# Fourteen remainders of converted weights on GpSimd instead of VectorE

## The chip, the cores and the metric

The kernel runs on one core of a Trainium2 chip. The metric is the device time of one execution in microseconds (us). TensorE does the matrix products, VectorE (DVE), ScalarE (ACT) and GpSimd (POOL) work on tiles in SBUF, SyncE (SP) issues the DMAs. VectorE and ScalarE also read PSUM, where TensorE writes.

## The reference

Channel attention over 6016 tokens of 256 channels, and after it two dense layers, each with a wide hidden part of 2048:

```
qn = q / (norm(q, axis=1) + 1e-6); kn = k / (norm(k, axis=1) + 1e-6)
a  = softmax(kn^T @ qn / tau)          # 256 x 256
x  = v @ a                             # 6016 x 256
h  = x @ w1_in;  g = elu(h);  x = g @ w1_out
h  = x @ w2_in;  g = silu(h); out = g @ w2_out
```

q, k and v are float32. The four weight matrices (256 x 2048 and 2048 x 256) are float64.

## The kernel before, in words

*Precision.* Each factor of a product is kept as two tiles: a high part, rounded to the type that TensorE takes at full rate (fp32r), and the remainder, the value less the high part. `product` issues three matmuls for one product: high x high, high x remainder, remainder x high, in this order, all into one PSUM bank (line 297). `split` (line 288) makes the pair: `copy(hi, src)` on ScalarE (line 256 in the profile), then `tt(lo, src, hi, subtract)` on VectorE (line 270). `products` (line 311) does the same for two products that share a bank.

*Conversion of the weights.* A float64 weight arrives as two 32-bit words. `in_f32` makes a float32 of them: two copies on ScalarE (tiles "cv" and "st"), then on VectorE two `tensor_scalar` operations (line 273, "cv<-cv"), a `scalar_tensor_tensor` (line 276, "cv<-st,cv") and an integer addition (line 270, shown as CUSTOM_DVE_ANT_0). `convert` then calls `split` with the float32 chunk of 128x512. The weights of layer one come in eight chunks of w_in ("w1i") and eight of w_out ("w1o"). Chunks 0 and 1 of w_in are split into corners of the tile "wo", the other six into "xs", all eight of w_out into "wo". So the remainders of layer one are `wo<-cv,wo` ten times and `xs<-cv,xs` six times. The weights of layer two are split by other functions (`put_by`, `second_weights`).

*Stages.* First the column norms and kn^T q are summed over all tokens while q and k are loaded (to about 41 us). Then the softmax, and the product of it with the chunks of w_in (`m_product`, `m_group`, line 311), which puts the attention into the weights of layer one. Tokens are then worked in groups of 1024 (the last of 896), all of layer one and then all of layer two, each group in eight steps `j` over the hidden part. In a step four units of 128x512 are made: `first_plain` in the first group (24 matmuls), a scheme with fewer products and more additions in all later ones. Each unit goes through the activation (`unit`, line 256 on ScalarE, lines 276 and 270 on VectorE) into a pair of tiles "gs", the last of which is the remainder `gs<-e,gs` on VectorE (where the pair lies in spare room of "wa", `wa<-e,wa`). `second` multiplies a unit with a chunk of w_out, six matmuls into the banks "y". In the first group (to about 160 us) the chunks of w_out and of w_in are converted as the steps need them: the conversions, the units and the products of the softmax with w_in run side by side there.

*Order.* All instructions are first put in a list by `do`, with an engine, a price from the table `COST` and the tiles they read and write. `in_order`, a planner, then writes one order for each engine by these prices and by the length of the way to the end; the engines run their orders strictly, with waits where tiles are shared. All DMAs go through SP's queue, but for some at the beginning and the end. GpSimd makes constants and the identity matrix in the first 1.3 us and nothing after.

Of the kernel before, what the change touches and what calls it, by code (L numbers as in the profile page):

```python
# [16 lines left out]
ALU = mybir.AluOpType  # L17
# [4 lines left out]
EARLY = ("w1i", 0), ("w1i", 1), ("w1o", 0), ("w1i", 2), ("w1i", 3)  # L22
# [21 lines left out]
    "PE": (0.0127, 1 / 2400, 0.22, 0.0),  # L44
    "ACT": (0.14, 1 / 1400, 0.18, 0.12),
    "DVE": (0.067, 1 / 960, 0.15, 0.19),
    "SP": (0.37, 0, 2.3, 0.0),
    "-": (0.0, 0, 0.0, 0.0),
}
# [2 lines left out]
V = namedtuple("V", "ap keys")  # L52
# [20 lines left out]
def real(ap):  # L73
    return ap.get() if isinstance(ap, Later) else ap
# [80 lines left out]
def channel_attention_elu_silu(  # L155
# [28 lines left out]
    nc = tc.nc  # L184
# [38 lines left out]
    def f32(ap):  # L223
        return ap.bitcast(F32)
# [6 lines left out]
    def do(engine, n, emit, reads, writes, times=1, far=0.0):  # L231
        fixed, each, late, own = DENSE if dense and engine == "ACT" else COST[engine]
        late += far
        ops.append(
            Op(
                engine,
                times * (fixed + each * n),
                late,
                own,
                emit,  # L240
                [k for v in reads if isinstance(v, V) for k in v.keys],
                [k for v in writes for k in v.keys],
                hot,
            )
        )

    def width(ap):
        return int(np.prod(ap.shape[1:]))

    def at(x):  # L250
        return real(x.ap) if isinstance(x, V) else x
# [14 lines left out]
    def copy(out, src, **kw):  # L266
        act(out, src, AF.Copy, **kw)

    def tt(out, a, b, op):
        do("DVE", width(out.ap), lambda: nc.vector.tensor_tensor(at(out), at(a), at(b), op), [a, b], [out])  # L270
# [14 lines left out]
        queue, engine = (nc.scalar, "ACT") if by == "ACT" else (nc.sync, "SP")  # L285
        do(engine, 0, lambda: queue.dma_start(at(out), at(src)), [src], [out], n if engine == "SP" else 2 + 3 * short, far)  # L286

    def split(hi, lo, src):
        copy(hi, src)
        tt(lo, src, V(f32(hi.ap), hi.keys), ALU.subtract)  # L290

    def product(out, lhs, rhs, start=True, stop=True, **kw):

# [90 lines left out]
    def wo_at(part, i):  # L384

        also = tuple(("eT", part, d) for d in range(CT)) if i == NP - 1 else ()
        if i in (5, 6):
            also = tuple(("w1i", part, x) for x in range(2))
        return V(wo[part][:, 2 * i : 2 * i + 2], (("wo", part, i), *also))

    def w1i_at(i, a, c, half=None):

        if i == 0:
            w = wo[a][:, 10:14].rearrange("p (c x) f -> p c (x f)", c=CT)
            return V(w[:, c], (("w1i", a, half),))
        x = 2 * ((i - 1) % 2)
        return V(xs[0][:, x : x + 2, a][:, c], (("x", x, a), ("x", x + 1, a)))
# [31 lines left out]
    def in_f32(name, i, *order, far=0.0, after=(), wait=()):  # L429


        raw = load(name, i, *order, far=far, after=after)
        low, high = src_of.pop((name, i))
        t = cvs.take()
        a, b = low.ap.shape[1:3]
        w = V(t.ap.rearrange("p (a b) -> p a b", a=a), t.keys)
        wi = V(w.ap.bitcast(I32), t.keys)
        copy(w, V(f32(high.ap), high.keys + wait), scale=2.0**-112)
        copy(low, V(low.ap.bitcast(U32), low.keys + wait), scale=2.0**-29)
        ts(w, w, TOP, -TOP, ALU.min, ALU.max)  # L440
        ts(wi, wi, 3, None, ALU.logical_shift_left)
        stt(wi, V(high.ap, high.keys), SIGN, wi, ALU.bitwise_and, ALU.bitwise_or)
        tt(V(flat(wi.ap), wi.keys), V(flat(wi.ap), wi.keys), V(flat(low.ap), low.keys), ALU.add)
        return w, raw

    def convert(name, i, *order, wait=(), far=LATE[0]):
        w, _ = in_f32(name, i, *order, far=far if order else 0.0, wait=wait)
        if name == "w1i":
            s = slice(i % 2 * HC, (i % 2 + 1) * HC)
            hi, lo = (w1i_at(i // 2, a, slice(None), i % 2) for a in range(2))  # L450
            split(V(hi.ap[:, :, s], hi.keys), V(lo.ap[:, :, s], lo.keys), w)
        else:
            split(wo_at(0, i), wo_at(1, i), w)

    def put_by(name, i, s):


        w, raw = in_f32(name, i, far=FAR, after=[("step", s - 1)])
        wf = V(flat(w.ap), w.keys)
        if name == "w2i":  # L460
            dma(V(w_dram[i], (("wid", i),)), wf)
            return
        both = V(raw.ap.rearrange("p (a x) -> p a x", a=2), raw.keys)
        half = lambda a: V(both.ap[:, a].bitcast(F32R), both.keys)
        split(half(0), half(1), wf)
        dma(V(wo_dram[i].rearrange("p a x r -> p a (x r)"), (("wod", i),)), both)
# [23 lines left out]
    with tc.manual_schedule():  # L490
# [87 lines left out]
        for i, (j0, nj) in enumerate(rows):  # L578
# [21 lines left out]
            if i == len(ENDS[0]):  # L600
                tau_ps = V(nsq.ap[:, 4:5], nsq.keys)
                matmul(tau_ps, V(ones, ()), V(small[:, 0:1], ("tau",)))
                recip(rtau, tau_ps)
        hot = 1
        convert(*EARLY[0], "order")
        hot = 0
        hot = 1
        convert(*EARLY[1], "order", far=LATE[1])
        hot = 0
        j0, nj0 = groups[0]  # L610
        for n in (1, 0):
            for b in range(4):
                s = slice(n * nj0 // 2, (n + 1) * nj0 // 2)
# [17 lines left out]
        for i in range(HELD[1] - 1, -1, -1):  # L631
            scores(last - i, (0,))
        hot = 0
        convert(*EARLY[2], "order")
        hot = 3
        x = V(nsq.ap[:, 0:4], nsq.keys)
# [617 lines left out]
```

## Time and profile before

| what | value |
|---|---|
| runs | 1037.50, 1037.96, 1038.38 us (median 1037.96) |
| profiled execution, span from first to last instruction | 1035.8 us |
| TensorE busy | 1030.4 us (99%) |
| VectorE busy | 825.1 us (80%) |
| ScalarE busy | 749.4 us (72%) |
| GpSimd busy | 0.7 us (0%) |
| granted TensorE clock | full speed throughout |

The span of the profiled execution is what the profile shows of its time; the median of the runs lies 2.2 us above it. Busy shares are means over stages: in 60 to 142 us VectorE is busy for 80.56 of 82 us, after 600 us for some 65 in 100. A group of matmuls in the timeline goes from the first one's start to the last one's end, and matmuls overlap, so twelve of them that follow each other at full rate take 2.88 us and not twelve times the duration of one. A group that holds a wait is longer than its like.

### The profile page before, as it was taken

Reading aid. Unit: us, or ns where it says so; the run is one execution under the profiler, and the core shown is the slowest. Engines: PE = TensorE matmul, PEld = TensorE weight load, DVE = VectorE, ACT = ScalarE, POOL = GpSimd, SP = SyncE. Lnnn points to the kernel's source line nnn. Section 1 sums busy time; section 2 is a strip of 40 time slices with the busy share of each in tenths; the row PEclk is TensorE's granted clock in tenths of the full one; section 3 lists DMA queues with packets and bytes.
Section 4 is the critical chain, followed back from the end, with each engine's and each line's share of the span. In section 5 each row is a group of like instructions: output and inputs, shape, how many; then the busy total and the mean of one; then the engine's idle time right before and its main releaser. Section 6 shows DMA issues by size and latency. Waiting matters only on the chain.

```text
span 1035.8 us, 13366 instructions
## 1 busy us (share of the span) xinstructions
PE 1030.4 (99%) x4734; PEld 872.4 (84%) x4734; DVE 825.1 (80%) x1401; ACT 749.4 (72%) x1410; POOL 0.7 (0%) x6
## 2 busy tenths in 40 slices
PE   9999999999999999999999999999999999999998
PEld 8888888888888888888998888998888888888887
DVE  6999999999989989989998866667566657657553
ACT  6799988989788888888897765565565556555543
POOL 0000000000000000000000000000000000000000
PEclk9999999999999999999999999999999999999999
DMA  9663332033032113013434003012003003001102
GB/s 379 220 173 113 112 71 102 1 72 112 18 75 103 51 46 102 31 42 122 135 97 156 11 1 82 1 41 37 1 4 78 1 1 82 1 1 22 20 1 41
DMA packets 112389, 71.38 MB, mean 69 GB/s; under 512 B 87874, under 2 KB 90562, under 8 KB 111682
## 3 DMA queue, kind: packets, MB, share of 16 engines
q1 hardware_dynamic: 109584, 68.96, 22.6%
q10 hardware_dynamic: 2738, 1.57, 0.5%
q8 instruction: 37, 0.61, 0.3%
q14 instruction: 30, 0.25, 0.1%
HBM read 49.81 MB, written 20.71 MB: 68 GB/s over the span
## 4 chain that ended last, share of the span: by engine, by line
PE 99%; ACT 0%; ACTq 0%; DVE 0%; issue 0%
PE y L297 50%; PE h L297 44%; PE y L324 4%; PE h L311 1%; PE h L324 0%; PE y L311 0%; PE h L329 0%; ACTq L286 0%; ACT big L256 0%; PE y L329 0%; ACT h L256 0%; ACT a L256 0%; DVE a L276 0%; DVE ones L491 0%; ACT e L256 0%
## 5 line engine op out<-in xcount | busy, mean ns | idle before, releaser
L297 PE MATMUL y<-gs,wo 128*128 128x512 f32 (+1 forms) x2196 | 520.5, 385 | 0.0
L297 PEld LDWEIGHTS y<-gs,wo 128*128 128x128 f32 x2196 | 411.8, 188 | 78.1 <-ACT e L256 0.8
L297 PE MATMUL h<-xs,wa 128*128 128x512 f32 (+1 forms) x1980 | 472.6, 385 | 0.0
L297 PEld LDWEIGHTS h<-xs,wa 128*128 128x128 f32 x1980 | 370.9, 188 | 68.5
L270 DVE TENSOR_TENSOR gs<-e,gs 128x512 fp32r<-128x512 f32 (+1 forms) x382 | 253.2, 676 | 90.9 <-ACT e L256 88.6
L270 DVE TENSOR_TENSOR h<-h,h 128x512 f32<-128x512 f32 (+1 forms) x352 | 228.0, 678 | 80.2 <-PE h L297 62.3
L256 ACT ACTIVATE e<-h 128x512 f32<-128x512 f32 (+2 forms) x383 | 225.5, 600 | 46.1 <-DVE h L270 43.5
L256 ACT ACTIVATE h<-h 128x512 f32<-128x512 f32 (+1 forms) x176 | 103.6, 589 | 136.8 <-PE h L297 136.7
L256 ACT ACTIVATE gs<-h 128x512 fp32r<-128x512 f32 (+1 forms) x192 | 116.5, 607 | 70.0 <-DVE h L270 37.7
L276 DVE SCALAR_TENSOR_TENSOR e<-e,h 128x512 f32<-128x512 f32 (+1 forms) x190 | 123.0, 671 | 18.2 <-ACT e L256 17.7
L256 ACT ACTIVATE e<-e 128x512 f32<-128x512 f32 (+1 forms) x192 | 114.0, 623 | 1.3
L256 ACT ACTIVATE gs<-e 128x512 fp32r<-128x512 f32 (+1 forms) x190 | 110.7, 624 | 1.6 <-DVE e L276 1.6
L270 DVE TENSOR_TENSOR xs<-big,xs 128x512 fp32r<-128x512 f32 (+1 forms) x77 | 50.2, 672 | 0.0
L256 ACT ACTIVATE xs<-big 128x512 fp32r<-128x512 f32 (+1 forms) x77 | 45.4, 623 | 1.0 <-DVE big L270 0.7
L270 DVE TENSOR_TENSOR sums<-sums 128x2048 f32<-128x2048 f32 (+3 forms) x17 | 29.4, 1727 | 7.2 <-ACT sums L256 6.2
L273 DVE TENSOR_SCALAR cv<-cv 128x512 f32<-128x512 f32 (+1 forms) x64 | 26.4, 422 | 0.6 <-ACT cv L256 0.3
L297 PEld LDWEIGHTS y<-wo,gs 128*128 128x128 f32 x192 | 24.7, 191 | 1.0
L297 PE MATMUL y<-wo,gs 128*128 128x256 f32 x192 | 25.1, 283 | 0.0
L256 ACT ACTIVATE cv<-st 128x512 f32<-128x512 f32 x32 | 21.4, 674 | 1.5 <-DMA st<-in_moe_w_in_dram 1.5
L324 PE MATMUL y<-ring 128*128 128x256 f32 x92 | 22.3, 395 | 0.0
L276 DVE SCALAR_TENSOR_TENSOR cv<-st,cv 128x512 int32<-128x512 int32 x32 | 21.9, 687 | 0.4
L270 DVE CUSTOM_DVE_ANT_0 cv<-st,cv 128x1024 uint16<-128x1024 uint16 x32 | 21.9, 686 | 0.0
(100 smaller groups left out, 369.6 us busy)
## 6 DMA issues: line engine op xcount, KB each, us to landing
st<-in_moe_w_in_dram SPq DMA_DIRECT2D x16, 512.0 KB, 3.9
st<-in_moe_w_out_dram SPq DMA_DIRECT2D x16, 512.0 KB, 3.8
yd<-e SPq DMA_DIRECT2D x20, 256.0 KB, 2.4
big<-yd SPq DMA_DIRECT2D x5, 1024.0 KB, 4.7
big<-in_v_dram SPq DMA_DIRECT2D x32, 128.0 KB, 3.5
wod<-st SPq DMA_DIRECT2D x8, 512.0 KB, 2.9
wo<-wod SPq DMA_DIRECT2D x8, 512.0 KB, 4.0
out_dram<-big SPq DMA_DIRECT2D x32, 128.0 KB, 2.9
```

The costliest lines, as they stand in the source:

```text
L256: nc.scalar.activation(at(out), at(src), func, **{k: at(x) for k, x in kw.items()}, **more)
L270: do("DVE", width(out.ap), lambda: nc.vector.tensor_tensor(at(out), at(a), at(b), op), [a, b], [out])
L273: do("DVE", width(out.ap) / 2, lambda: nc.vector.tensor_scalar(at(out), at(a), at(s1), at(s2), *op), [a, s1, s2], [out])
L276: emit = lambda: nc.vector.scalar_tensor_tensor(at(out), at(a), at(s), at(b), op0, op1)
L297: nc.tensor.matmul(at(out), at(lhs[a]), at(rhs[b]), start=start and a + b == 0, stop=stop and a == 1, **kw)
L311: nc.tensor.matmul(at(out), at(both[n][0][a]), at(both[n][1][b]), start=(n, a, b) == (0, 0, 0), stop=(n, a) == (1, 1),)
L324: emit = lambda: nc.tensor.matmul(at(out), at(lhs), at(rhs), start=start, stop=stop, **kw)
```

## The change

`split` gets a flag with which the remainder is made by GpSimd; `convert` sets it for all chunks of w_out of layer one, and for the chunks of w_in other than the first two. The planner's table gets a price for GpSimd. The operation, its inputs and its output are the same.

```diff
     "DVE": (0.067, 1 / 960, 0.15, 0.19),
+    "POOL": (0.2, 2.2 / 1000, 0.2, 0.12),
     "SP": (0.37, 0, 2.3, 0.0),
...
-    def split(hi, lo, src):
+    def split(hi, lo, src, pool=False):
         copy(hi, src)
-        tt(lo, src, V(f32(hi.ap), hi.keys), ALU.subtract)
+        if pool:
+            high = V(f32(hi.ap), hi.keys)
+            do("POOL", width(lo.ap), lambda: nc.gpsimd.tensor_tensor(at(lo), at(src), at(high), ALU.subtract), [src, high], [lo])
+        else:
+            tt(lo, src, V(f32(hi.ap), hi.keys), ALU.subtract)
...
         if name == "w1i":
             s = slice(i % 2 * HC, (i % 2 + 1) * HC)
             hi, lo = (w1i_at(i // 2, a, slice(None), i % 2) for a in range(2))
-            split(V(hi.ap[:, :, s], hi.keys), V(lo.ap[:, :, s], lo.keys), w)
+            split(V(hi.ap[:, :, s], hi.keys), V(lo.ap[:, :, s], lo.keys), w, (name, i) not in EARLY[:2])
         else:
-            split(wo_at(0, i), wo_at(1, i), w)
+            split(wo_at(0, i), wo_at(1, i), w, True)
```

The four numbers of a price are a fixed part, a part for each element of a row, and what is added until another engine, or the same engine, can use the result, in us. `EARLY[:2]` are chunks 0 and 1 of w_in.

## Rows read from the trace of the kernel before

**Rows 1.** The page, busy us of each engine (share of the span), instructions
```profile
PE 1030.4 (99%) x4734; PEld 872.4 (84%) x4734; DVE 825.1 (80%) x1401; ACT 749.4 (72%) x1410; POOL 0.7 (0%) x6
```

**Rows 2.** The page, the chain that ended last, by engine
```profile
PE 99%; ACT 0%; ACTq 0%; DVE 0%; issue 0%
```

**Rows 3.** TensorE's timeline, 48 to 53 us: start, us, what, count
```profile
48.43 1.06 PE L311 MATMUL h<-wo 128*128 128x256 f32 x6
...
52.15 0.88 PE L311 MATMUL h<-wo 128*128 128x256 f32 x6
```

**Rows 4.** TensorE's timeline, groups of twelve matmuls between 63 and 160 us
```profile
63.91 3.53 PE L297 MATMUL y<-gs,wo 128*128 128x512 f32 x12
67.28 2.90 PE L311 MATMUL h<-xs,wo 128*128 128x512 f32 x12
70.02 2.88 PE L297 MATMUL y<-gs,wo 128*128 128x512 f32 x12
...
75.46 2.88 PE L297 MATMUL y<-gs,wo 128*128 128x512 f32 x12
...
118.98 2.88 PE L297 MATMUL y<-gs,wo 128*128 128x512 f32 x12
...
156.38 3.42 PE L297 MATMUL y<-gs,wo 128*128 128x512 f32 x12
```

**Rows 5.** Stretch: PE, PEld, DVE, ACT, POOL busy (count), clock, DMA share, GB/s
```profile
60.00:142.00 82.00, 81.99 (x360) 67.13 (x360) 80.56 (x148) 78.63 (x149) 0.00 (x0) 1.00 0.40 113
```

**Rows 6.** Waits, 60 to 68 us: who waited for whom, us, times, longest
```profile
PEld y L297 <- DVE gs L270: 0.4, 1, 0.4
PEld y L297 <- ACT h L256: 0.4, 1, 0.4
PEld y L297 <- DVE e L276: 0.2, 1, 0.2
```

**Rows 7.** VectorE's timeline: two successive starts, and remainders of units 2, 19, 33
```profile
60.07 0.69 DVE L270 TENSOR_TENSOR wo<-cv,wo 128x512 fp32r<-128x512 f32 x1
60.67 0.69 DVE L270 TENSOR_TENSOR gs<-e,gs 128x512 fp32r<-128x512 f32 x1
...
65.02 0.68 DVE L270 TENSOR_TENSOR gs<-e,gs 128x512 fp32r<-128x512 f32 x1
...
110.62 0.70 DVE L270 TENSOR_TENSOR gs<-e,gs 128x512 fp32r<-128x512 f32 x1
...
153.89 0.69 DVE L270 TENSOR_TENSOR gs<-e,gs 128x512 fp32r<-128x512 f32 x1 [0.24 <-ACT gs L256]
```

**Rows 8.** Remainders of weights, 35 to 170 us: ns min/median/max, first and last start
```profile
L270 DVE TENSOR_TENSOR wo<-cv,wo x10: 681/686/697, 46.3 to 138.5; 128x512 fp32r<-128x512 f32 x10
L270 DVE TENSOR_TENSOR xs<-cv,xs x6: 661/690/701, 62.6 to 112.4; 128x512 fp32r<-128x512 f32 x6
```

**Rows 9.** GpSimd by form: busy us, mean ns; and the last in its timeline
```profile
masks.py:199 POOL TENSOR_SCALAR_AFFINE_SELECT ident<-ident 128x128 f32<-128x128 f32 x1 | 0.3, 294 | 0.1
masks.py:197 POOL MEMSET ident<- 128x128 f32 x1 | 0.2, 206 | 0.3 <-POOLq L1235 0.3
...
L1235 POOL MEMSET const-float32-0.0<- 128x1 f32 x1 | 0.1, 99 | 0.2 <-issue 0.2
...
1.01 0.29 POOL masks.py:199 TENSOR_SCALAR_AFFINE_SELECT ident<-ident 128x128 f32<-128x128 f32 x1
```

**Rows 10.** ScalarE's timeline: high parts of two weight chunks
```profile
65.41 0.65 ACT L256 ACTIVATE xs<-cv 128x512 fp32r<-128x512 f32 x1
...
73.97 0.64 ACT L256 ACTIVATE wo<-cv 128x512 fp32r<-128x512 f32 x1
```

**Rows 11.** VectorE by line, 60 to 142 us: busy us, mean ns, idle before
```profile
L270 DVE TENSOR_TENSOR gs<-e,gs 128x512 fp32r<-128x512 f32 x28 | 18.7, 688 | 0.0
L273 DVE TENSOR_SCALAR cv<-cv 128x512 f32<-128x512 f32 (+1 forms) x24 | 9.8, 425 | 0.4 <-ACT cv L256 0.3
L270 DVE CUSTOM_DVE_ANT_0 cv<-st,cv 128x1024 uint16<-128x1024 uint16 x12 | 8.3, 689 | 0.0
L276 DVE SCALAR_TENSOR_TENSOR cv<-st,cv 128x512 int32<-128x512 int32 x12 | 8.1, 686 | 0.0
...
L270 DVE TENSOR_TENSOR xs<-big,xs 128x512 fp32r<-128x512 f32 x5 | 3.4, 687 | 0.0
```

## The prediction
> **What bounds the kernel now.** I read the page's busy times first, then the chain of waits, then busy times by stretch, then single engines in order of time where TensorE's order is broken. The busy times say that TensorE works for 1030.4 of 1035.8 us [rows 1], and the chain that ended last is 99% TensorE [rows 2]. The reader is to see in this that an engine beside TensorE can win or lose time only where TensorE waits for it. Such waits are partly hidden in "busy", since a matmul that is held up shows as a longer group. So I compared groups of equal shape. Before 60 us six matmuls take 1.06 us in one place and 0.88 in another [rows 3], and the like of this adds up, by my estimate from these two, to 0.8 us at most. Twelve matmuls of 128x512 take 2.88 us wherever nothing holds them, and 3.53 in the group at 63.91 and 3.42 in the one at 156.38 [rows 4]: 0.65 and 0.54 us lost. With 0.8 that is 2.0 us, and it is all that the change can win: 0.19% of the time.
>
> The stretch in which the change works is the first group of layer one, 60 to 142 us. There TensorE is busy 81.99 of 82.00 us, VectorE 80.56 and ScalarE 78.63 [rows 5]. All three are full, so VectorE's load matters if it grows, although it ends nothing on its own now. What stands between it and TensorE is a lead. Units are used in the order in which they are made; counted from the first, the group at 70.02 uses units 3 and 4, the one at 75.46 units 5 and 6, the one at 118.98 units 19 and 20, and the one at 156.38 units 33 and 34. Unit 2's remainder ends at 65.02 + 0.68 = 65.70, and TensorE wants it in the stretched group at 63.91 and waits 0.4 us for it [rows 6, 7]: no lead. Unit 19's ends at 111.32; its second matmul, the first that reads it, starts at 118.98 + 0.23 = 119.21: 7.9 us of lead. Unit 33's ends at 154.58 and is wanted at 156.61: 2.0 us [rows 4, 7]. So delay on VectorE costs time before some 77 us and again near 155 us, and hardly between.
>
> **The change part by part.** *Removed from VectorE:* 14 of the 16 remainders of layer-one weights: all eight of w_out and six of w_in. They are the ten rows into "wo" less the two of the first w_in chunks, which stay, and the six into "xs" [rows 8]. One takes 0.686 to 0.690 us, but VectorE starts the next instruction 0.60 us later (60.07 to 60.67, [rows 7]), so one frees 0.60 and fourteen free 8.4 us. Nearly all of it lies beside a full TensorE and shortens nothing. On the path are the two remainders at 60.07 and near 62.6, ahead of unit 2: 1.2 us of VectorE time in front of a stall of 0.65. The stall has three parts: 0.2 for a VectorE read of a bank, 0.4 for the remainder of unit 2, 0.4 for a ScalarE copy [rows 6]. The third stays, and is what is late next; it overlaps the others, so I count 0.25 us as won. The loss at 156.38 follows evacuations by ScalarE, for which the change does nothing: 0.
>
> *Added on GpSimd:* 14 subtractions of 128x512 with two inputs. The trace has no such row. GpSimd's own rows are a write of 128x128 in 206 ns, one of 128x1 in 99, and an operation with one input on 128x128 in 294 [rows 9]. Over 127 more elements the write grows by 0.84 ns each; the input adds 88 ns on 128, or 0.69 ns each. Two inputs: 0.10 + 512 x (0.84 + 2 x 0.69)/1000 = 1.24 us. The lower bound is VectorE's own 0.69; the upper is two passes with one input each, 2 x (0.10 + 512 x 1.53/1000) = 1.77 us. I take 1.24. Fourteen are 17.4 us on an engine that has been idle since 1.3 us, with nothing queued behind them.
>
> *Added wait:* the remainder comes later to TensorE by 1.24 - 0.69 = 0.55 us. Where there is room this costs nothing. Two places are tight. The remainder near 66.2 is of the chunk read by the twelve matmuls at 67.28, from the second, 67.51; ScalarE's copy ends at 66.06 [rows 10], so GpSimd ends at 67.3: in time by 0.2. The remainder for the group at 75.46 is wanted by its third matmul at 75.91; the copy ends at 73.97 + 0.64 = 74.61, GpSimd at 75.85: in time by 0.06. At the bounds the two cost 0 and (67.83 - 67.51) + (76.38 - 75.91) = 0.8 us. I take 0.1.
>
> *Shared use of SBUF by the two engines.* No row shows GpSimd beside VectorE, so it can cost nothing, or stop VectorE for all 17.4 us. At the one end VectorE is 8.4 us lighter, at the other 9.0 us heavier. What this is worth is set by the lead: only the four subtractions before 77 us count in full, so the ends are -0.65 (no more than the stall) and 4 x (1.24 - 0.60) = 2.6 us, and then what the later ten, 6.4 us, leave over a lead of 5 to 8 us. I take 0, for half of a subtraction's time in VectorE's way, 0.62, is what one frees, 0.60.
>
> [...]
>
> *Moved:* the order. All engines' order is written by one planner, which gets a price for GpSimd (0.2 + 512 x 2.2/1000 = 1.33 us) and 0.6 us less on VectorE fourteen times. It will bring other work forward, and DMA issues on SP with it. The kernel has almost no idle TensorE time under this planner after 160 us, so I take 0; a bound from what this planner's order lost in one place is +-0.65.
>
> *Sum:* -0.25 + 0.1 + 0 + 0 = -0.15 on a span of 1035.8. The median of the runs shown is 1037.96, 2.2 above the span; that part stays. Forecast: **1037.8 us**, no change that can be told.
>
> **The rivals.** *First, VectorE is held by GpSimd (slower).* While GpSimd subtracts, VectorE's next instruction waits for it. Price at full length: 2.6 us before 77 us, plus 6.4 less a lead of some 5.6 = 0.8 near 155: 3.4 us, 1041.4. It decides against the forecast from the point where a subtraction holds VectorE for more than the 0.60 it frees. [...] Against it: an instruction that GpSimd meets already running holds GpSimd instead. 20%.
>
> *Second, GpSimd is held by VectorE and the remainders come late.* Each of the tight ones waits for one VectorE instruction of 0.69 and takes up to 1.77: 2 x 0.69 + 0.8 = 2.2 us, 1040.0. For it: VectorE leaves no gap of its own there. Against: the planner sees a price of 1.33 and can put other matmuls ahead. 9%.
>
> *Third, the stalls go.* The lighter VectorE, and an order that suits ScalarE too, remove most of the 2.0 us: 1036.3. For it: both the early losses lie behind VectorE work. Against: the ScalarE parts. 13%.
>
> *Fourth, the change does not do what it says:* the planner fills VectorE's freed time with other conversions so that its load at the tight places is what it was. That gives the forecast's time as well, and is in its chance.
>
> **How the numbers follow.** The forecast has 58%, from 1037.0 to 1039.0. With the rivals the range goes from 1036.4 (most of the third) to 1041.0 (most of the first). A measurement of this kernel can tell 0.2%, 2.1 us, from no change: 1035.9 and 1040.0 are the limits. Faster: only the end of the third rival, 3%. Slower: most of the first, half of the second, and 2% for an order that turns out badly: 21%. Same: 76%.
>
> **What would show it.** Right, if GpSimd has 14 subtractions near 1.24 us between 55 and 142 us, VectorE's busy time there falls by some 8 us less what it lost by waiting, the group that uses unit 2 is shorter than 3.53 us, and TensorE's groups of twelve stay at 2.88. The first rival would show as VectorE instructions much longer than 0.69 us while GpSimd works, and stretched matmul groups before 80 and near 155 us; the second as GpSimd instructions of 1.8 us and more, and weight loads that wait for GpSimd. The prediction is wrong if TensorE's groups are stretched by over 2 us together, or if a stall appears after 160 us, where I count on none.

## The result, and the profile after

The changed kernel takes 1044.74 us (five runs, 1044.53 to 1045.21) against 1037.79 for the kernel before (five runs): ratio 1.0068, 95% interval 1.0056 to 1.0081. The forecast was 1037.8 with a range up to 1041.0, and 21% for slower. The time lies outside the range.

The page after, busy us of each engine, answers to [rows 1]:

```profile
PE 1033.6 (99%) x4734; PEld 871.7 (84%) x4734; DVE 827.3 (79%) x1387; ACT 749.6 (72%) x1410; POOL 26.6 (3%) x20
```

VectorE has 14 instructions less, and yet 2.2 us more of busy time than the 825.1 of before. The freed 14 x 0.60 = 8.4 us are gone, so others of its instructions must have become longer, by about 8.4 + 2.2 = 10.6 us over the span. GpSimd has 14 instructions more and 25.9 us more, 1.85 each, not 1.24. The chain that ended last, which answers to [rows 2], has other engines in it now:

```profile
PE 90%; DVE 5%; ACT 3%; issue 2%; ACTq 0%; DVEq 0%
```

The stretch of 60 to 142 us, with the columns of [rows 5], shows TensorE without work for 3.6 of 82 us, where it was full before:

```profile
60.00:142.00 82.00, 78.40 (x338) 62.39 (x337) 79.19 (x131) 73.62 (x139) 24.56 (x14) 1.00 0.39 110
```

GpSimd's timeline of the changed kernel (start, us, what, count, idle time before it) shows what one subtraction takes:

```profile
74.68 1.30 POOL L293 TENSOR_TENSOR wo<-cv,wo 128x512 fp32r<-128x512 f32 x1 [6.82 <-ACT wo L257]
...
107.87 4.70 POOL L293 TENSOR_TENSOR wo<-cv,wo 128x512 fp32r<-128x512 f32 x1 [8.50 <-ACT wo L257]
112.52 3.46 POOL L293 TENSOR_TENSOR xs<-cv,xs 128x512 fp32r<-128x512 f32 x2
121.67 1.35 POOL L293 TENSOR_TENSOR wo<-cv,wo 128x512 fp32r<-128x512 f32 x1 [5.69 <-ACT wo L257]
...
140.15 3.02 POOL L293 TENSOR_TENSOR wo<-cv,wo 128x512 fp32r<-128x512 f32 x1 [8.72 <-ACT wo L257]
```

1.30 us is its length when nothing is in its way, and 4.70 the longest. VectorE's timeline of the same kernel beside it:

```profile
110.72 0.68 DVE L277 SCALAR_TENSOR_TENSOR cv<-st,cv 128x512 int32<-128x512 int32 x1
111.32 0.67 DVE L277 SCALAR_TENSOR_TENSOR e<-e,h 128x512 f32<-128x512 f32 x1
111.92 1.19 DVE L271 CUSTOM_DVE_ANT_0 cv<-st,cv 128x1024 uint16<-128x1024 uint16 x1
...
117.39 0.68 DVE L271 TENSOR_TENSOR gs<-e,gs 128x512 fp32r<-128x512 f32 x1
117.99 0.68 DVE L277 SCALAR_TENSOR_TENSOR e<-e,h 128x512 f32<-128x512 f32 x1
...
121.78 1.79 DVE L271 TENSOR_TENSOR gs<-e,gs 128x512 fp32r<-128x512 f32 x1
```

From 107.87 on VectorE runs one instruction after the other (the last stands here) that reads two tiles in SBUF or is a `tensor_scalar`; none is longer than usual, and GpSimd does not get on. At 111.32 comes `e<-e,h`, whose second input is a PSUM bank. GpSimd's subtraction ends at 107.87 + 4.70 = 112.57, 1.25 after that start, so it ran beside it; and the next VectorE instruction, of two SBUF inputs, ends at 113.11, 0.54 after GpSimd. At 121.78 GpSimd was first: VectorE's 0.69 became 1.79. Eleven VectorE instructions end 0.3 to 1.1 us beyond their usual length beside a subtraction, 9.3 us in all (what makes up the rest of the 10.6 was not traced); the `e<-e,h` and the transpose that run beside one do not. In these rows each engine holds the other, for the whole of an instruction.

What this does to TensorE is seen in its waits, 100 to 130 us (who waited for whom, us, times, longest), where there were none before, and in its timeline:

```profile
PEld h L302 <- DVE a L277: 1.8, 1, 1.8
...
PEld h L316 <- DVE e L277: 1.4, 2, 1.0
PE h L302 <- DVE a L277: 1.4, 1, 1.4
...
PE h L302 <- DVE e L277: 0.6, 1, 0.6
```

```profile
64.96 0.97 PE L302 MATMUL y<-gs,wo 128*128 128x512 f32 x3 [0.65 <-DVE e L277]
66.16 2.38 PE L302 MATMUL y<-gs,wo 128*128 128x512 f32 x9 [0.23 <-DVE e L277]
...
118.72 3.32 PE L316 MATMUL h<-xs,wo 128*128 128x512 f32 x12 [0.56 <-DVE e L277]
121.87 2.88 PE L302 MATMUL y<-gs,wo 128*128 128x512 f32 x12
125.38 0.70 PE L302 MATMUL h<-xs,a 128*128 128x512 f32 x2 [0.62 <-DVE e L277]
127.48 1.20 PE L302 MATMUL h<-xs,a 128*128 128x512 f32 x4 [1.40 <-DVE a L277]
```

None of these waits is for GpSimd. But for the last, of 1.40 us, the matmuls wait for VectorE's `e<-e,h`, or `e<-e,y`: not for the result of the unit, but for the PSUM bank that this instruction reads and that the next product is to overwrite. The group at 118.72 starts 0.05 us after the `e<-e,h` that ends at 118.66. The last waits for a result: the remainder `a` of the weights with the softmax. Comparing the starts of successive matmuls, TensorE lost 7.4 us more than before over the span: 1.1 between 60 and 80 us, 4.1 between 100 and 130, 1.1 between 150 and 170, 0.8 between 200 and 340, and the rest in steps of less than 0.3.

The same place before, in VectorE's and TensorE's timelines:

```profile
112.96 1.29 DVE L276 SCALAR_TENSOR_TENSOR e<-e,h 128x512 f32<-128x512 f32 x2
```

```profile
116.26 2.88 PE L311 MATMUL h<-xs,wo 128*128 128x512 f32 x12
```

The two reads end at 113.65 and 114.25, and the two halves of the group, which overwrite those two banks, start at 116.26 and 117.62: a lead of 2.6 and 3.4 us, while the units' lead was 5.7 and 7.9 there. After the change the banks' lead is 0.05, and the units' still 5.4 to 7.3.

A third link is shorter still. Before, the remainder `a` ends at 119.93 + 0.48 = 120.41, and the third matmul of the group that uses it starts at 122.15, a lead of 1.7 us:

```profile
119.93 0.48 DVE L276 SCALAR_TENSOR_TENSOR a<-h,small,a 128x256 fp32r<-128x256 f32 x1
```

```profile
121.70 1.52 PE L297 MATMUL h<-xs,a 128*128 128x512 f32 x6
```

After the change that matmul starts at 127.48, just behind the remainder. Of the 4.1 us lost between 100 and 130 us, the banks account for 2.0 and the remainders of the weights with the softmax for 2.1.

### The profile page after: what moved, and what is told of

It is laid out like the page before. It is cut to its first block, busy times and chain, and to the rows that moved or that the text cites. A ratio compares the mean times of both kernels' runs of the same rounds, so it can differ in the third digit from the quotient of the medians.

```text
span 1043.2 us, 13378 instructions
## 1 busy us (share of the span) xinstructions
PE 1033.6 (99%) x4734; PEld 871.7 (84%) x4734; DVE 827.3 (79%) x1387; ACT 749.6 (72%) x1410; POOL 26.6 (3%) x20
## 4 chain that ended last, share of the span: by engine, by line
PE 90%; DVE 5%; ACT 3%; issue 2%; ACTq 0%; DVEq 0%
PE y L302 45%; PE h L302 39%; PE y L329 4%; ACT e L257 1%; DVE gs L271 1%; DVE e L277 1%; DVE cv L277 1%; DVE cv L274 1%; PE h L329 0%; DVE h L271 0%; ACT gs L257 0%; ACT xs L257 0%; DVE xs L271 0%; DVE cv L271 0%; ACT cv L257 0%
## 5 line engine op out<-in xcount | busy, mean ns | idle before, releaser
L271 DVE TENSOR_TENSOR gs<-e,gs 128x512 fp32r<-128x512 f32 (+1 forms) x382 | 257.2, 686 | 91.9 <-ACT e L257 88.4
```

## The experiments

Theory A: the two engines hold each other, and VectorE's lost time reaches TensorE through the banks in an order that has no room for it. B: the planner's new order is what costs, without any hold. C: the remainders come too late. Where a run is in the order of before, or in the new order, VectorE and ScalarE run the instructions of the kernel before, or of the changed one, in the same order, but for the remainders. The edits are in the function `split` unless said otherwise. Times of before: 1037.63 us for the first four, 1037.66 for the last four.

**Order of before, GpSimd makes the remainders.** The planner is told nothing:

```diff
-            do("POOL", width(lo.ap), lambda: nc.gpsimd.tensor_tensor(...), [src, high], [lo])
+            do("DVE", width(lo.ap), lambda: nc.gpsimd.tensor_tensor(...), [src, high], [lo])
```

> The order of the kernel before (the planner prices the 14 remainders as VectorE work of 0.60 us), but GpSimd makes them. Theory A, the hold: a subtraction on GpSimd stops VectorE for about 0.66 us (9.3 us over 14 in the trace after), and VectorE's lost time reaches TensorE through the PSUM banks that it has to read before they are written again; here the order has left 0.60 us for each, so nearly all of the loss goes: 1037.5 to 1039.5 us. Theory B, the order: the planner's new order is the worse one in itself, the hold harmless: 1036.5 to 1038. Theory C, lateness: the remainders come too late for TensorE, since VectorE holds GpSimd for up to 3.4 us; here the planner expects them 0.7 us sooner still, so it is as slow as the changed kernel or slower: 1043 to 1047.

Measured: 1038.62 us, ratio 1.0011 (1.0002 to 1.0020). Of the 7 us of loss 1 us is left, with the same 14 subtractions on the same engine. Its timeline of TensorE:

```profile
65.54 2.61 PE L302 MATMUL y<-gs,wo 128*128 128x512 f32 x9 [0.85 <-DVE e L277]
...
117.54 2.88 PE L316 MATMUL h<-xs,wo 128*128 128x512 f32 x12
120.26 2.88 PE L302 MATMUL y<-gs,wo 128*128 128x512 f32 x12
122.98 1.52 PE L302 MATMUL h<-xs,a 128*128 128x512 f32 x6
```

The stall near 65 us is longer than before and those of 100 to 130 us are gone. So C falls as the cause of the 7 us: here the remainders are expected sooner than by the new order, and one wait of TensorE for GpSimd comes of it, near 77 us, which costs about 0.4 us. Moving the work to GpSimd costs little by itself, if VectorE's order keeps the 0.60 us of each remainder free.

**New order, VectorE makes the remainders.**

```diff
-            do("POOL", width(lo.ap), lambda: nc.gpsimd.tensor_tensor(...), [src, high], [lo])
+            do("POOL", width(lo.ap), lambda: nc.vector.tensor_tensor(...), [src, high], [lo])
```

> The order of the changed kernel on every engine, but VectorE makes the 14 remainders, each where the planner put the one of GpSimd. Theory A: VectorE carries 14 x 0.60 = 8.4 us that the order has no room for, in place of the 9.3 us for which it was held: about as slow as the changed kernel, 1042.5 to 1045.5 us. Theory B (a bad order): the same, 1042.5 to 1045.5. Theory C: remainders are no longer late, at most in time with VectorE: 1038 to 1040.

Measured: 1042.55 us, 1.0045 (1.0031 to 1.0058), at the lower edge of what A and B expected. GpSimd does nothing, and two thirds of the loss are there. TensorE's waits, 100 to 166 us, are for the same instructions:

```profile
PEld h L302 <- DVE a L277: 1.8, 1, 1.8
...
PEld h L302 <- DVE e L277: 1.2, 2, 1.0
PEld h L316 <- DVE e L277: 0.9, 2, 0.4
```

So this order has no room on VectorE for 8.4 us, whatever takes them.

**New order, GpSimd only writes.** The remainders are left out, but for one column of each half:

```diff
+            def emit():
...
+                for _ in range(3):
+                    nc.gpsimd.memset(out, 0.0)
+                nc.gpsimd.tensor_tensor(at(lo)[edge], a[edge], b[edge], ALU.subtract)
...
```

> The order of the changed kernel; GpSimd fills each remainder with zeros three times (writes alone, some 1.4 us in all) and then subtracts one column of each half, so the wait on ScalarE's copy and TensorE's wait on GpSimd stay; the remainders are left out but for these columns. Theory A: writes do not stop VectorE, which is now 8.4 us lighter in an order made for that: 1036.5 to 1038.5 us, VectorE's instructions at their usual length while GpSimd works. Theory B: the order is what costs, so 1043 to 1046. Theory C: GpSimd is not held any more, so its results are in time: 1036.5 to 1039; if it is held by VectorE in writing too, 1042 or more, with GpSimd's fills of over 0.6 us in the trace.

Measured: 1039.11 us, 1.0013 (1.0004 to 1.0022); above A's range by 0.6, and 5.6 below the changed kernel with the same order. B falls for the most part: with the fills, but without holds by subtractions, the order costs 1.5 us, near 65 us and in three places after 190 us (VectorE carries less here than in any kernel that makes all the remainders), and TensorE's groups between 100 and 160 us are whole:

```profile
117.32 2.88 PE L324 MATMUL h<-xs,wo 128*128 128x512 f32 x12
120.04 2.88 PE L310 MATMUL y<-gs,wo 128*128 128x512 f32 x12
122.76 1.52 PE L310 MATMUL h<-xs,a 128*128 128x512 f32 x6
```

GpSimd's small subtractions and its fills (which start before ScalarE's copy here, as they read nothing), and VectorE beside the fills at 110.73:

```profile
105.36 3.53 POOL L299 TENSOR_TENSOR wo<-cv,wo 128x2 fp32r<-128x2 f32 x1 [6.96 <-ACT wo L257]
...
110.60 0.20 POOL L299 TENSOR_TENSOR xs<-cv,xs 128x2 fp32r<-128x2 f32 x1
110.73 1.69 POOL L298 MEMSET xs<- 128x512 f32 x3
```

```profile
110.72 0.69 DVE L271 TENSOR_TENSOR gs<-e,gs 128x512 fp32r<-128x512 f32 x1
111.33 0.69 DVE L271 TENSOR_TENSOR big<-big 128x512 f32<-128x512 f32 x1
111.94 0.77 DVE L274 TENSOR_SCALAR cv<-cv 128x512 f32<-128x512 f32 x1
```

Instructions with two SBUF inputs keep their 0.69 us beside a write; the `tensor_scalar` goes from 0.42 to 0.77. Five are so lengthened, 2.1 us in all, and a part of the 1.5 us may be theirs. So the traces of this run and of the changed kernel have two inputs beside a subtraction (1.79 us), two inputs beside a fill (0.69) and `tensor_scalar` beside a fill (0.77).

**Pieces of 128 columns.** The changed kernel, each subtraction in four:

```diff
...
+                for c in range(out.shape[1]):
+                    for h in range(2):
+                        s = slice(h * out.shape[2] // 2, (h + 1) * out.shape[2] // 2)
+                        nc.gpsimd.tensor_tensor(out[:, c, s], a[:, c, s], b[:, c, s], ALU.subtract)
...
```

> The changed kernel with each subtraction on GpSimd in four pieces of 128 columns (some 0.40 us each by the rows of 1.30 us for 512 columns and 0.10 us for the smallest instruction). Theory A with a hold for each instruction: VectorE loses less at a time but four times, 0.1 to 0.4 us each, 0.4 to 1.6 us for a remainder: 1041 to 1048 us. If the two engines share SBUF without a lock for the whole instruction, pieces change nothing but the fixed 0.3 us: 1044 to 1046. Theory C: GpSimd gets in less often between VectorE's instructions and is later: 1046 or more.

Measured: 1044.08 us, 1.0062 (1.0050 to 1.0075). The time is within what both readings expected. The trace tells more: the hold goes by the piece, for each of the two `gs<-e,gs` beside the four at 74.64 is some 0.26 us longer, and 27 VectorE instructions together 6.0, against 9.3 for whole subtractions. But the four take 2.62 us where one whole took 1.30, and GpSimd's lateness now reaches TensorE by a way round. ScalarE waits for GpSimd to be done with the tile "cv", and VectorE for ScalarE:

```profile
114.84 0.66 ACT L257 ACTIVATE cv<-st 128x512 f32<-128x512 f32 x1 [2.50 <-POOL xs L299]
```

```profile
115.53 0.43 DVE L274 TENSOR_SCALAR cv<-cv 128x512 f32<-128x512 f32 x1 [1.89 <-ACT cv L257]
```

So C has a part here, which no wait of TensorE names. In the changed kernel this wait of ScalarE is 0.5 us, and VectorE does not stand idle for it. Cutting up the work is no way out.

**Order with room, and a later result.** The planner prices a remainder as 0.70 us of VectorE and expects it 1.45 us after:

```diff
+            do("DVE", width(lo.ap) + 100, lambda: nc.gpsimd.tensor_tensor(...), [src, high], [lo], far=1.3)
```

> GpSimd makes all 14 remainders; the planner prices each as 0.70 us of VectorE's time and expects the result 1.45 us after that, so its order has room for the hold and for the late result. Theory A (what costs is that VectorE is held in an order without room for it): the loss of 100 to 160 us is absent, as with the order of before, and the early stalls near 65 us decide: 1037.3 to 1039.3 us. If the late result is what cost 1 us with the order of before (TensorE waited 0.28 us for GpSimd once), it comes to 1037 to 1038; if any order made for GpSimd is a bad one, 1040 or more.

Measured: 1040.03 us, 1.0023 (1.0015 to 1.0032), 0.7 above A's range, and just inside that of the last reading, that any order made for GpSimd is a bad one. The loss of 100 to 130 us is absent, as A has it, but this third order has stalls of its own: 1.05 us for `e<-e,y` near 65 us, and some 1 us near 150 and 160. An order with room is not yet a good one, and whether another made for GpSimd would be is open.

**The ten late ones alone, and the first four alone, in the order of before.** The first four are those before 80 us; `do("DVE", ...)` is as in the first run:

```diff
+FIRST = ("w1o", 0), ("w1i", 2), ("w1i", 3), ("w1o", 1)
...
+            split(wo_at(0, i), wo_at(1, i), w, (name, i) not in FIRST)    # the ten late ones
+            split(wo_at(0, i), wo_at(1, i), w, (name, i) in FIRST)        # the first four
```

> The order of the kernel before; GpSimd makes only the ten remainders after 80 us, VectorE the first four again. With all 14 on GpSimd in this order TensorE's extra stalls lay near 65 and 76 us and none after 80. Theory A with room: these ten cost nothing, and the stall of 0.54 us near 157 us, which was gone with all 14, may go: 1037.0 to 1038.0 us. If the hold costs wherever it falls: 1038.3 or more.

> The order of the kernel before; GpSimd makes only the four remainders before 80 us. The counterpart of the run with the ten late ones: if the place decides, all of the loss of some 1.0 us is here, with stalls of 1.3 to 1.6 us near 65 and 0.4 near 76: 1038.3 to 1039.3 us. If the loss is spread over all 14: 1037.7 to 1038.1.

Measured: 1037.84 us for the ten, 1.0002 (0.9993 to 1.0010), and 1038.67 for the four, 1.0008 (0.9999 to 1.0017). In the order of before the place decides: ten subtractions under a lead cost nothing that can be told (in the trace a wait for a bank near 91 us costs 0.4, and the loss near 157 us is gone), and four near 65 and 76 us about 1 us, though that interval just touches no change. TensorE's timeline with the four:

```profile
65.87 2.62 PE L303 MATMUL y<-gs,wo 128*128 128x512 f32 x9 [0.85 <-DVE e L278]
...
77.33 0.96 PE L303 MATMUL y<-gs,wo 128*128 128x512 f32 x3 [0.17 <-POOL wo L294]
```

The second line is one of the few waits for GpSimd in any run: the place that the prediction called tight.

**New order, the first four without the hold.** As in the run that only writes, for those four; the ten late ones subtract:

```diff
...
+                if pool > 1:
+                    nc.gpsimd.tensor_tensor(at(lo), at(src), at(high), ALU.subtract)
+                    return
...
```

> The order of the changed kernel; GpSimd makes the ten remainders after 80 us as the changed kernel does, and for the first four it fills the tiles with zeros and subtracts two columns, so these four are left out but for that. Theory A: TensorE's loss of 4 to 5 us between 100 and 165 us stays, since it comes from the ten holds in an order that has no room on VectorE, and 0.3 us near 65 us goes: 1042.5 to 1044.5 us. If the delay that the first four put on VectorE was handed on to the places after 100 us: 1039 to 1041.

Measured: 1044.37 us, 1.0062 (1.0049 to 1.0075), in A's range. In the new order it is the ten late ones that cost. In steps: 1037.7 before; +1.5 by the new order with fills alone; +5.3 by the ten holds (1044.37 less 1039.11); +0.4 by the first four. The steps are differences of whole times, and where TensorE loses the time varies: in this run's trace the granted clock is 0.50 from 127 to 130 us (0.98 as the mean of 60 to 165 us); what lowers it is not shown. That costs 1.4 us there, and most of the loss of 150 to 170 us is absent in return; two of the five runs have a mean clock of 1.000 and take 1044.09 and 1044.37 us.

## Why the prediction was wrong

*What bounds the kernel* stands: no version tried was faster than the kernel before, which agrees with a bound of 2 us, though no run tests the bound itself. The 0.25 us counted as won near 64 us was not won: between 60 and 80 us TensorE lost 1.1 us more than before.

*The lead* is the step that failed: "delay on VectorE costs time before some 77 us and again near 155 us, and hardly between". Between 100 and 130 us TensorE lost 4.1 us. The prediction measured the lead at one link from VectorE to TensorE, the remainders of the units, 7.9 us near 119, and let the ten late subtractions disappear under it. VectorE also sets TensorE free, since it reads the banks; the prediction had such a read in its rows, 0.2 us near 64 [rows 6]. That lead was 2.6 to 3.4 us at 116 us [rows 4 have the group that follows]. And VectorE makes the remainders of the weights with the softmax, with a lead of 1.7 us at 122. Both were shorter than the holds, of which 6.8 us fell before 117 us. At the group at 118.72 the sum can be followed: the `e<-e,h` that it waits for ends 5.0 us later than before, TensorE itself is 1.7 us later by then, and 5.0 less 1.7 less the lead of 2.6 is 0.7, the delay that the group adds.

*The freed 8.4 us* were set against the hold, 0.60 freed by 0.62 lost, with 0 as the outcome. The size was nearly right: 9.3 us over 14, 0.66 each. But the freed time was not there to be set against it. The planner had spent it: by the group at 118.72 VectorE had made four instructions for the tokens of the next group (`big<-big` twice, `big<-big,big`, `xs<-big,xs`) that stand later in the order of before. In the run that only writes VectorE is busy for 36.9 of the 37 us from 80 to 117, so the holds came on top of a VectorE that was full. In that run the banks' lead near 117 us is 2.5 to 2.8 us, about that of before, but the lead of the remainder `a` is down to 0.6: it ends at 122.62, for a matmul at 123.21 of the group at 122.76.

```profile
122.14 0.48 DVE L277 SCALAR_TENSOR_TENSOR a<-h,small,a 128x256 fp32r<-128x256 f32 x1
```

This is the fourth rival, which I had counted as harmless, together with the first; neither decides alone. The order of before with the same subtractions costs 1.0, the new order with fills alone 1.5, the two together 7.0.

*The first rival* had the mechanism and its point of decision, "more than the 0.60 it frees", which was passed only in name; its price of 3.4 was too low since it took the same lead.

*GpSimd's length* was 1.24 by my estimate and 1.30 where nothing held it. The second rival's mechanism is there (4.70, 3.02 us), but TensorE never waited for GpSimd in the changed kernel, and ScalarE once, for 0.5 us.

*The order*, taken as 0 with a bound of 0.65, cost up to 1.5 (the run that only writes, with what its fills took from `tensor_scalar`). Every order tried has stalls of 0.6 to 1.7 us near 65 us; why the new one's are longer was not tried, and stays open.

## What to carry to other kernels

When work is taken off an engine that is full beside a full TensorE, ask what the scheduler does with the freed time before setting it against the cost: run the new placement under the old order, and the old placement under the new order, and the price of each comes apart from what they cost together. Measure an engine's lead at every link to TensorE, the banks that it frees as well as each kind of result that it delivers; the shortest counts. GpSimd was no free helper for VectorE where both read SBUF: 14 subtractions took 9.3 us from it, and freed 8.4. No version tried here beats the kernel before.

## What the hardware showed

In the trace of the changed kernel a VectorE instruction with two SBUF inputs and a GpSimd subtraction excluded each other whole: 0.69 became 1.79 us, and GpSimd's 1.30 became 4.70 while VectorE ran such instructions and `tensor_scalar` back to back; there it got in only beside one that reads PSUM. Its own size did not help it: a subtraction of two columns, 0.20 us when free, took 3.53 in the same place of the run that only writes. At 82.65 us it got in after one VectorE instruction without a PSUM input (1.75 us in all); what decides this is not shown. GpSimd's fills of 128x512 (1.69 us for three) left two-input instructions at 0.69 and took a `tensor_scalar` of 0.42 to between 0.77 and 0.88.
